# A schedule that counts buffer reuse and holds its DMA queue short, early buffers for the decay inputs, and a first batch mixed in single fp32 products

## The chip, the cores and the metric

The kernel runs on one core of a Trainium2 chip. The metric is device time in microseconds (us) for one execution. The engines are TensorE (PE, with its weight loads PEld), VectorE (DVE), ScalarE (ACT), GpSimd (POOL) and SyncE (SP), which here issues every DMA.

## The reference

Three blocks follow one another, for 4 batches, 768 time steps and 384 channels (8 heads of 48).

```python
# 1. attention with a decayed state, for each batch and head
f = 1.0 / (1.0 + np.exp(-f_logit))
for t in range(S):
    state = f[:, :, t, :, None] * state + np.einsum('bhd,bhe->bhde', k[:, :, t], v[:, :, t])
    y[:, :, t] = np.einsum('bhd,bhde->bhe', q[:, :, t], state)
# 2. token mix with phases
theta = x @ w_theta
zr, zi = x * np.cos(theta), x * np.sin(theta)
y = np.einsum('ts,bsd->btd', w_tok_r, zr) + np.einsum('ts,bsd->btd', w_tok_i, zi)
u = x + y
x = u + np.maximum(u @ w_ch, 0.0)
# 3. gated block with a spatial product
h = np.maximum(x @ w_in, 0.0); u, v = halves of h
v_n = (v - mean(v)) / sqrt(var(v) + 1e-6)
out = (u * (einsum('ts,bsd->btd', w_spatial, v_n) + b_spatial)) @ w_out
```

The token weights (w_tok_r, w_tok_i) arrive as 64-bit numbers and are turned into fp32 on the chip.

## The kernel before, in words

**Decays** (`dense`). The channels of one batch make three groups of 128 rows, so there are twelve groups, f0, k0, q0 to f11, k11, q11. For each group the kernel loads f, k and q (128x768), forms 1 + exp(-f) on ACT, takes a running product over chunks of 64 steps on DVE (the scan `icp<-f,one`), then multiplies k and q by what ACT makes of it by Ln and Exp. Before the scan a memset on GpSimd clears the first column of every chunk. The f tiles have one buffer (`BUFS`), the k and q tiles two each.

**Attention** (`att_load`, `att_k`, `att_w`, `att_s`, `att_x`). A unit is a pair of heads. Its rows are copied by DMA from the k and q tiles into `kp` and `qa`, and small products follow: scores `psc`, chunk states `pw`, outputs `px`. Two units have buffers at a time, and batch 0 has units 0 to 3.

**Phases** (`p1_theta`, `p1_z`). Per 128 time steps: theta (`pth`) on PE, its reduction on DVE, two sines on ACT, and z = x cos, x sin.

**Token mix** (`p1_acc`). `acc` sums z times token tiles over six blocks c of 128 steps, once for each half (th) of the output steps. With fp32r operands a product is made as three products over split operands (high x high, high x low, low x high); each operand's low part costs one ACT copy and one DVE subtraction (`split`). The token tiles of a batch are twelve, 128x768 each. In the first batch they are loaded raw (768 KB), decoded (one ACT and three DVE operations), and kept in DRAM for the later batches, either whole (`tkd`) or as two split parts (`tkp`). For b = 0 and c < MIX1 = 3 nothing is split: one fp32 product, which the profile counts as two records, stands for the three. Then z has one buffer in use and its second (`z10`, `z11`, `z12` of tags `z1c`) is idle until the second batch.

**Channel product** (`p1_u`, `p1_h`) follows each half, then block 3 for each batch (`pv`, `pu`, `pg`, `po`), all in triple products.

**What sets the order.** Up to the end of block 2 all instructions are recorded first. `Plan.schedule` then gives each engine a fixed order: a list schedule with a cost for each instruction, in which a unit takes a free buffer and waits for the earliest one. `late` computes from the end backwards by when each instruction must start, and these due times are the priorities of the next of four rounds; the best round's order is imposed. On the chip each engine runs its list strictly in order, SP its DMA issues too.

Names in rows and orders: `f1_221` is the f tile of group 1, `kp0`, `qa00` and `qa01` belong to even units and `kp1`, `qa10`, `qa11` to odd ones, `ws` is a raw load, `wb` a decoded tile that is split afterwards, `tk0` and `tk1` are token tiles (high or whole, and low).

Of the kernel before, what the change touches and what calls it, by code (L numbers as in the profile page):

```python
# [10 lines left out]
F32 = mybir.dt.float32  # L11
# [10 lines left out]
P = 128  # L22
B, H, S, D = 4, 8, 768, 48
# [3 lines left out]
NC = S // C  # L27
# [5 lines left out]
LIMIT = float(2.0**40)  # L33
TWO_PI = 2.0 * math.pi

THETA1, MIX1 = 2, 3

PARTS = 4
BUFS = {"f": 1, "k": 2, "q": 2}

FILL = 30

# [13 lines left out]


MODE, HOP, ISSUE, RATE, NARROW, LAND, SLACK = 0.1, 0.11, 0.6, 310e3, 160e3, 1.2, 0.05
ROUNDS = 4


# [27 lines left out]
class Plan:  # L89
# [111 lines left out]
            u[0].touch = {x for o in u for x in {b.t for b in o.out + o.src} if x in self.use}  # L201

    def schedule(self):
        free = {k: [0.0] * n for k, n in self.size.items()}
        turn = {k: 0 for k in self.order}
        left = {t: len(s) for t, s in self.use.items()}
        last = {t: 0.0 for t in self.use}
        queue = {e: [] for e in "TVAGQ"}
        for u in self.units:
            queue[u[0].e].append(u)  # L210
        for q in queue.values():
            q.sort(key=lambda u: (u[0].pri, u[0].i))
        now = {e: 0.0 for e in "TVAGQ"}
        end, seq, picks = {}, {e: [] for e in "TVAGQ"}, {}
        dma, mode, func, cols = 0.0, None, None, {}

        def ready(u):
            t, o = 0.0, u[0]
            for d, same in o.deps:
                x = end.get(d)  # L220
                if x is None:
                    return None
                t = max(t, x - HOP if same else x)
            for k, xs in o.need:
                f = free[k]
                if len(f) < len(xs):
                    return None
                i = turn[k]
                if self.order[k][i : i + len(xs)] != xs:
                    return None  # L230
                t = max(t, sorted(f)[len(xs) - 1])
            return t

        for _ in self.units:
            best = None
            for e in "TVAGQ":
                c = None
                for u in queue[e]:
                    r = ready(u)
                    if r is None:  # L240
                        continue
                    s = max(r, now[e])
                    if c is None or s < c[0] - 1e-9:
                        c = (s, u)
                    if s <= now[e] + SLACK:
                        break
                if c is not None and (best is None or c[0] < best[0]):
                    best = (c[0], e, c[1])
            s, e, u = best
            queue[e].remove(u)  # L250
            for k, xs in u[0].need:
                for _ in xs:
                    free[k].remove(min(free[k]))
                turn[k] += len(xs)
            t = s
            for o in u:
                o.start = t
                if e == "T":
                    if o.mode != mode and mode is not None:
                        t += MODE  # L260
                    mode = o.mode
                    if o.mode[1] < P and o.name != "transpose":
                        c = o.out[0].p[0]
                        x = max(t, cols.get(c, 0.0))
                        cols[c] = x + 2 * o.cost
                        t = x + 0.006
                        end[o] = cols[c] + HOP + 0.07
                    else:
                        t = max([t] + list(cols.values())) + o.cost
                        cols = {}  # L270
                        end[o] = t + HOP + 0.07
                elif e == "Q":
                    t += o.cost
                    dma = max(dma, t + 0.5) + o.bytes / o.rate
                    end[o] = dma + LAND
                else:
                    if o.func == "sin":
                        t += 0.1 + (1.28 if func != "sin" else 0)
                    func = o.func or func
                    t += o.cost  # L280
                    end[o] = t + HOP
                seq[e].append(o)
                for x in {b.t for b in o.out + o.src}:
                    if x in left:
                        left[x] -= 1
                        last[x] = max(last[x], end[o])
                        if not left[x]:
                            free[self.tag[x]].append(last[x])
            now[e] = max([t] + list(cols.values())) if e == "T" else t
        return max(now["T"], now["V"]), seq, end  # L290

    def late(self, seq, end):
        late = {}
        after = {}
        for e in "T":
            for x, y in zip(seq[e], seq[e][1:]):
                after[x] = y
        succ = {}
        for u in self.units:
            for d, same in u[0].deps:  # L300
                succ.setdefault(d, []).append((u[0], same))
        fin = max(end.values())
        for o in sorted(self.ops, key=lambda o: -o.start):
            t = fin
            for s, same in succ.get(o, ()):
                if s in late:
                    t = min(t, late[s] - (0 if same else HOP))
            if o in after and after[o] in late:
                t = min(t, late[after[o]])
            late[o] = t - (end[o] - o.start if o.e == "Q" else o.cost)  # L310
        return late

    def run(self):
        self.prepare()
        best = None
        for _ in range(ROUNDS):
            t, seq, end = self.schedule()
# [42 lines left out]
class Kernel:  # L360
# [105 lines left out]
    def dense(self, b, g):  # L466
        V, A, G = self.V, self.A, self.G
        self.ln_exp()
        n, t = 3 * b + g, {}
        self.dn[n] = t  # L470
        for x in ("f", "k", "q"):
            t[x] = self.a2.tile([P, S + NC], F32, name=f"{x}{n}", tag=x, bufs=BUFS[x])
            self.Q.dma_start(out=t[x][:, 0:S], in_=self.a[x].rearrange("u r t -> (u r) t")[P * n : P * n + P])
        f, k, q, cx = t["f"][:, 0:S], t["k"][:, 0:S], t["q"][:, 0:S], t["k"][:, S:]
        icp, cw = self.icp, self.cw
        fc = f.rearrange("p (c t) -> p c t", t=C)
        fs = self.a2.tile([P, NC], F32, name=f"fs{n}", tag="fs")
        self.act(f, f, AF.Exp, scale=-1.0)
        A.activation(f, f, AF.Copy, bias=1.0)
        V.reciprocal(fs, fc[:, :, 0])  # L480
        G.memset(fc[:, :, 0:1], 0.0)
        V.tensor_tensor_scan(icp, f, self.one.rearrange("p c t -> p (c t)"), 0.0, op0=ALU.mult, op1=ALU.add)
        G.tensor_copy(self.ge[:, n, :], icp[:, C - 1 : S : C])
        self.act(cw, icp, AF.Ln)
        self.act(cw, cw, AF.Exp, scale=-1.0)
        yield
        V.tensor_tensor(k, k, icp, op=ALU.mult)
        V.tensor_tensor(icp, cw, icp, op=ALU.mult)
        V.scalar_tensor_tensor(cw, icp, 2.0, cw, op0=ALU.subtract, op1=ALU.mult, reverse0=True)
        yield  # L490
        V.tensor_tensor(q, q, cw, op=ALU.mult)
        ce = cw.rearrange("p (c t) -> p c t", t=C)[:, :, C - 1]
        G.tensor_tensor(cx[:, 0 : NC - 1], ce[:, 0 : NC - 1], fs[:, 1:NC], op=ALU.mult)
        G.memset(cx[:, NC - 1 : NC], 0.0)
        yield
# [539 lines left out]
    def run(self):  # L1035
# [21 lines left out]
        dense = lambda b, g: self.ahead(self.dense(b, g), 1000 if g or b else 0)  # L1057
        w = self.p1_weights()
        run(dense(0, 0))
        run(take(w, NJ))  # L1060
        p = self.bank("pt")
        for _ in range(FILL):
            self.T.matmul(p[:, 0:P], lhsT=self.ident, rhs=self.ident, start=True, stop=True)
        self.att_k(0, 0)
        run(merge((dense(0, 1), 9), (self.att_pe(0, X[0]), 6)))
        self.att_k(0, 1)
        run(merge((dense(0, 2), 9), (self.att_pe(1, X[0]), 6)))
        self.att_k(0, 2)
        run(pe(2))
# [95 lines left out]
```

## Time and profile before

| | us |
|---|---|
| median of 3 runs | 646.95 |
| lowest and highest run | 645.7, 651.62 |
| profiled execution, first to last instruction (its span) | 642.1 |
| PE busy in it | 605.7 (94%) |
| DVE busy in it | 427.4 (67%) |
| ACT busy in it | 346.0 (54%) |

The profiled execution has no time of its own beside its span; the fastest run is 3.6 us over that span, the median 4.9 us. Shares of busy time are averages over stages with different limits: the profile is to be read by stretches of 20 us, and in each by which engine the others wait for.

### The profile page before, as it was taken

To read this page: it belongs to the slowest core of one execution; us is meant where nothing else is said; L and a number is where in the kernel's file an instruction comes from. 1 tells how busy PE (TensorE), PEld (TensorE's weight loads), DVE (VectorE), ACT (ScalarE), POOL (GpSimd) and SP (SyncE) were. 2 spreads that over 40 slices of the span, in tenths; PEclk is the share of its full clock that TensorE was granted. 3 is DMA by queue.
4 is the path that set the end of the run, shared out by engine and by line. 5 is a ranking of instruction groups with operands and counts; after the bars stand their busy time and mean duration, and the time that the engine had idled before them with its cause. 6 is when DMAs were issued, how large, how long until landed. Compare 5 with 4: busy or idle time off the path is not lost.

```text
span 642.1 us, 12784 instructions
## 1 busy us (share of the span) xinstructions
PE 605.7 (94%) x5140; PEld 558.4 (87%) x5140; DVE 427.4 (67%) x757; ACT 346.0 (54%) x637; POOL 28.7 (4%) x76
## 2 busy tenths in 40 slices
PE   9577988899999999999799999999999999999996
PEld 8466657678899998999799998999899989999996
DVE  3898799995979977776697525775745174518250
ACT  3666886646887678865675204633541263126211
POOL 5110001000002000010000000000000000000000
PEclk9668996999999999999999999999999999999999
DMA  8787667996968999365665634341010100020002
GB/s 264 233 245 232 230 198 222 318 319 195 330 213 255 313 310 243 120 215 177 203 223 191 215 102 160 90 134 55 19 53 22 66 10 24 1 75 1 1 1 79
DMA packets 40963, 102.05 MB, mean 159 GB/s; under 512 B 5696, under 2 KB 11840, under 8 KB 40896
## 3 DMA queue, kind: packets, MB, share of 16 engines
q1 hardware_dynamic: 40896, 101.15, 50.0%
q8 instruction: 42, 0.69, 0.4%
q14 instruction: 25, 0.20, 0.1%
HBM read 71.17 MB, written 20.45 MB: 143 GB/s over the span
## 4 chain that ended last, share of the span: by engine, by line
PE 79%; DVE 8%; DMA 5%; ACT 4%; issue 1%; POOL 1%; SPq 0%; DVEq 0%; ACTq 0%; POOLq 0%
PE acc L339 19%; PE pg L339 16%; PE pu L339 8%; PE po L339 8%; PE pv L339 8%; PE pth L339 5%; PE hh L339 5%; PE px L339 4%; PE psc L339 3%; PE pt L339 2%; DVE icp L339 2%; PE pw L339 1%; DMA f<-f_dram 1%; DMA xs<-x2d 1%; DMA tkd<-wb 1%
## 5 line engine op out<-in xcount | busy, mean ns | idle before, releaser
L339 PE MATMUL acc<-tk,z 128*128 128x384 f32 x828 | 169.8, 357 | 0.8 <-DVE xt L339 0.8
L339 PEld LDWEIGHTS acc<-tk,z 128*128 128x128 f32 x828 | 144.1, 189 | 10.9 <-DVE xt L339 1.3
L339 PE MATMUL pg<-wp,vn 128*128 128x384 f32 x576 | 100.5, 334 | 0.0
L339 PEld LDWEIGHTS pg<-wp,vn 128*128 128x128 f32 x576 | 99.9, 188 | 0.0
L339 ACT ACTIVATE gt<-g 128x384 fp32r<-128x384 f32 x32 | 16.8, 527 | 63.4 <-DVE g L339 63.4
L339 PE MATMUL pu<-x,wi 128*128 128x384 f32 x288 | 50.7, 334 | 0.0
L339 PE MATMUL po<-wo,gt 128*128 128x384 f32 x288 | 50.6, 336 | 0.0
L339 PEld LDWEIGHTS pu<-x,wi 128*128 128x128 f32 x288 | 50.1, 188 | 0.3
L339 PEld LDWEIGHTS po<-wo,gt 128*128 128x128 f32 x288 | 50.0, 188 | 0.0
L339 PE MATMUL pv<-wi,x 128*128 128x512 f32 x216 | 49.8, 390 | 0.0
L339 PEld LDWEIGHTS pv<-wi,x 128*128 128x128 f32 x216 | 40.5, 188 | 8.3
L339 PE MATMUL hh<-uT,wc 128*128 128x384 f32 x216 | 42.0, 342 | 3.3 <-DVE sn L339 3.1
L339 DVE BATCH_NORM_STATS2 st<-vv 128x6 f32<-128x512 f32 x24 | 16.5, 692 | 42.5 <-ACT vv L339 42.5
L339 PEld LDWEIGHTS psc<-qa,kp 64*64 64x64 f32 x768 | 28.7, 150 | 16.1 <-issue 12.0
L339 PE MATMUL psc<-qa,kp 64*64 64x64 f32 x768 | 32.2, 238 | 11.0 <-DVE qa L339 5.3
L339 DVE TENSOR_TENSOR qa<-psc,mask 64x384 f32<-64x384 f32 x64 | 35.5, 555 | 10.0 <-PE psc L339 8.5
L339 PEld LDWEIGHTS hh<-uT,wc 128*128 128x128 f32 x216 | 37.5, 188 | 5.1 <-DVE sn L339 3.4
L339 PE MATMUL px<-vs,qa 128*64 128x48 f32 x768 | 35.5, 253 | 5.6 <-ACT vs L339 3.9
L339 PEld LDWEIGHTS px<-vs,qa 128*64 128x64 f32 x768 | 31.8, 159 | 10.2 <-ACT vs L339 4.8
L339 DVE TENSOR_TENSOR g<-pg,bs 128x384 f32<-128x384 f32 x32 | 17.7, 557 | 27.1 <-PE pg L339 27.0
L339 ACT ACTIVATE vs<-cb 64x528 f32<-64x528 f32 x24 | 23.8, 990 | 14.1 <-DVE cb L339 13.9
L339 ACT ACTIVATE sn<-sn 128x384 f32<-128x384 f32 x48 | 24.5, 516 | 7.8 <-DVE sn L339 7.5
(111 smaller groups left out, 914.6 us busy)
## 6 DMA issues: line engine op xcount, KB each, us to landing
tk<-tkp SPq DMA_DIRECT2D x48, 384.0 KB, 4.4
ws<-tok_dram SPq DMA_DIRECT2D x12, 768.0 KB, 5.7
tkp<-tk SPq DMA_DIRECT2D x20, 384.0 KB, 5.2
f<-f_dram SPq DMA_DIRECT2D x12, 384.0 KB, 4.7
k<-k_dram SPq DMA_DIRECT2D x12, 384.0 KB, 6.6
q<-q_dram SPq DMA_DIRECT2D x12, 384.0 KB, 7.1
vn<-vu_dram SPq DMA_DIRECT2D x16, 288.0 KB, 5.8
vs<-va_dram SPq DMA_DIRECT2D x32, 144.0 KB, 5.1
```

The lines of the kernel that those rows point to most:

```text
L339: r = f(*a, **k)
```

## The change

1. `MIX1` goes from 3 to 6: in the first batch all six blocks of both halves use single fp32 products. No z and no token tile is split in that batch, all twelve decoded token tiles go whole to DRAM, and all twelve are split, and their parts stored, in the second batch.
2. `EARLY`: f1, f2, k2 and q2 get their tiles in the second z buffers, which are idle now through the first batch. They no longer wait for f0's buffer, or for k0's and q0's.
3. The memset before the scan moves from GpSimd to DVE.
4. `schedule` remembers which tile a buffer was taken from, and `late` counts the user of a buffer as a successor of the instructions of its previous tile.
5. `LEAD`: the schedule does not place a DMA before its modelled queue is within 1.5 us of empty. This is a rule of the planner alone; nothing on the chip enforces it.

```diff
-THETA1, MIX1 = 2, 3
+THETA1, MIX1 = 2, 6
+EARLY = {("f", 1): "z10", ("f", 2): "z11", ("k", 2): "z12", ("q", 2): "z13"}
+LEAD = 1.5
...
-                c = None
+                c, at = None, max(now[e], dma - LEAD) if e == "Q" else now[e]
...
-                    free[k].remove(min(free[k]))
+                    f = min(free[k])
+                    free[k].remove(f)
+                    self.took.append((f[1], u[0]))
...
+        for t, o in self.took:
+            for d in self.use.get(t, ()):
+                succ.setdefault(d, []).append((o, False))
...
-            t[x] = self.a2.tile([P, S + NC], F32, name=f"{x}{n}", tag=x, bufs=BUFS[x])
+            w = S + NC if x == "k" else S
+            if (x, n) in EARLY:
+                t[x] = self.c1.tile([P, w], F32, name=f"{x}{n}", tag=EARLY[x, n])
+            else:
+                t[x] = self.a2.tile([P, w], F32, name=f"{x}{n}", tag=x, bufs=BUFS[x])
...
-        G.memset(fc[:, :, 0:1], 0.0)
+        V.memset(fc[:, :, 0:1], 0.0)
```

The plan changes the order on every engine. On SP, at the start of the program, the loads before, from the second on:

```order
L339 DMA k0_140<-k_dram 128x768
L339 DMA q0_142<-q_dram 128x768
L339 DMA k1_223<-k_dram 128x768
L339 DMA vn0_102<-vu_dram 128x576
L339 DMA q1_225<-q_dram 128x768
L339 DMA vs0_100<-va_dram 64x576 x2
L339 DMA vn1_103<-vu_dram 128x576
L339 DMA vs1_101<-va_dram 64x576 x2
L339 DMA ws_160<-wt_dram 128x768
L339 DMA ws_167<-wt_dram 128x768
L339 DMA f1_221<-f_dram 128x768
```

and now:

```order
L348 DMA k0_140<-k_dram 128x768
L348 DMA f1_221<-f_dram 128x768
L348 DMA q0_142<-q_dram 128x768
L348 DMA k1_223<-k_dram 128x768
L348 DMA vn0_102<-vu_dram 128x576
L348 DMA q1_225<-q_dram 128x768
L348 DMA f2_370<-f_dram 128x768
L348 DMA vs0_100<-va_dram 64x576 x2
L348 DMA k2_372<-k_dram 128x768
L348 DMA kp0_104<-k0_140 48x780 x2
```

f1 moves from the fourteenth issue to the third, f2 and k2 come before the first unit's copies, and the theta weights (`wt`) go behind them.

On DVE, at the start, from the end of group 0's decays on, before:

```order
L339 TENSOR_TENSOR q0_142<-q0_142,cw_99 128x768
L339 TENSOR_SCALAR ft0_159<-ws_160 128x384
L339 SCALAR_TENSOR_TENSOR ft0_159<-ws_160,ft0_159 128x384 x2
L339 TENSOR_SCALAR ft1_166<-ws_167 128x384
L339 SCALAR_TENSOR_TENSOR ft1_166<-ws_167,ft1_166 128x384 x2
L339 RECIPROCAL fs1_227<-f1_221 128x12
L339 SCALAR_TENSOR_TENSOR icp_98<-f1_221,one_95 128x768
L339 TENSOR_TENSOR k1_223<-k1_223,icp_98 128x768
L339 TENSOR_TENSOR qa00_106<-psc_249,mask_91 64x384
L339 TENSOR_TENSOR qa01_107<-psc_249,mask_91 64x384
```

and now:

```order
L348 SCALAR_TENSOR_TENSOR cw_99<-icp_98,cw_99 128x768
L348 RECIPROCAL fs1_227<-f1_221 128x12
L348 MEMSET f1_221 128x12
L348 SCALAR_TENSOR_TENSOR icp_98<-f1_221,one_95 128x768
L348 TENSOR_TENSOR q0_142<-q0_142,cw_99 128x768
L348 TENSOR_TENSOR k1_223<-k1_223,icp_98 128x768
L348 TENSOR_TENSOR icp_98<-cw_99,icp_98 128x768
L348 SCALAR_TENSOR_TENSOR cw_99<-icp_98,cw_99 128x768
L348 TENSOR_TENSOR q1_225<-q1_225,cw_99 128x768
L348 RECIPROCAL fs2_376<-f2_370 128x12
L348 MEMSET f2_370 128x12
L348 SCALAR_TENSOR_TENSOR icp_98<-f2_370,one_95 128x768
```

The decays of groups 0, 1 and 2 stand directly behind one another, and the decoding of the theta weights (`ft`) comes after them.

On DVE, late in the first half of the first batch's mix (`tk0_978` is now the token tile of block 3, `tk0_987` was it), before:

```order
L339 TENSOR_SCALAR wb_989<-ws_990 128x768
L339 SCALAR_TENSOR_TENSOR wb_989<-ws_990,wb_989 128x768 x2
L339 TENSOR_TENSOR z13_798<-sn_790,z03_797 128x768
L339 TENSOR_TENSOR sn_811<-sn_811,X0_135 128x768
L339 TENSOR_TENSOR tk1_988<-wb_989,tk0_987 128x768
```

and now:

```order
L348 TENSOR_TENSOR z04_815<-sn_808,X0_135 128x768
L348 TENSOR_TENSOR z05_828<-sn_821,X0_135 128x768
L348 TENSOR_TENSOR wc1_81<-wb_848,wc0_80 128x384
L348 RECIPROCAL fs4_910<-f4_904 128x12
L348 MEMSET f4_904 128x12
L348 SCALAR_TENSOR_TENSOR icp_98<-f4_904,one_95 128x768
L348 TENSOR_TENSOR k4_906<-k4_906,icp_98 128x768
L348 TENSOR_SCALAR tk0_978<-ws_979 128x768
L348 SCALAR_TENSOR_TENSOR tk0_978<-ws_979,tk0_978 128x768 x2
```

The two subtractions of each block (for z and for the token tile) are gone, and the decode writes the token tile itself, of which there are three buffers, where it wrote `wb`, of which there is one.

## Rows read from the trace of the kernel before

**Rows 1.** The page's busy times: us, share of the span, instructions.

```profile
span 642.1 us, 12784 instructions
PE 605.7 (94%) x5140; PEld 558.4 (87%) x5140; DVE 427.4 (67%) x757; ACT 346.0 (54%) x637; POOL 28.7 (4%) x76
```

**Rows 2.** Stretches: length, PE, PEld, DVE, ACT, POOL busy (count), clock, DMA, GB/s.

```profile
0.00:20.00 20.00, 15.34 (x108) 14.99 (x108) 8.68 (x12) 8.10 (x11) 9.31 (x27) 1.00 0.85 249
38.77:65.07 26.30, 21.12 (x407) 18.58 (x410) 23.05 (x34) 17.02 (x36) 1.46 (x6) 0.81 0.78 244
65.07:118.72 53.65, 46.82 (x425) 34.98 (x417) 48.30 (x65) 40.69 (x68) 3.78 (x8) 0.90 0.73 233
118.72:167.41 48.69, 48.06 (x564) 37.92 (x564) 40.19 (x58) 28.79 (x52) 1.49 (x6) 1.00 0.88 276
...
200.00:220.00 20.00, 19.81 (x264) 17.92 (x264) 18.87 (x25) 15.77 (x24) 2.47 (x7) 1.00 0.94 280
220.00:240.00 20.00, 19.86 (x329) 18.23 (x325) 14.98 (x22) 13.04 (x26) 1.72 (x6) 1.00 1.04 314
```

**Rows 3.** Timeline of DVE: start, us, operation, out<-in, count [idle before <-releaser].

```profile
5.64 0.23 DVE L339 RECIPROCAL fs<-f 128x12 f32<-128x12 f32 x1 [5.64 <-ACT f L339]
8.60 1.76 DVE L339 TENSOR_TENSOR_SCAN icp<-f,one 128x768 f32<-128x768 f32 x1 [2.74 <-POOL f L339]
...
20.14 0.23 DVE L339 RECIPROCAL fs<-f 128x12 f32<-128x12 f32 x1 [0.94 <-ACT f L339]
...
37.81 0.96 DVE L339 TENSOR_TENSOR q<-q,cw 128x768 f32<-128x768 f32 x1
...
65.07 0.55 DVE L339 SCALAR_TENSOR_TENSOR sn<-sn,pth 128x384 f32<-128x384 int32 x1 [0.24 <-ACT sn L339]
...
69.01 0.96 DVE L339 TENSOR_TENSOR z<-sn,X 128x768 f32<-128x768 f32 x1 [2.99 <-ACT sn L339]
...
118.72 1.48 DVE L339 TENSOR_TENSOR xt<-acc,xt 128x384 f32<-128x384 f32 x3
```

**Rows 4.** Timeline of ACT, the first group's two passes over f.

```profile
3.89 1.72 ACT L339 ACTIVATE f<-f 128x768 f32<-128x768 f32 x2 [1.79 <-DMA f<-f_dram]
```

**Rows 5.** The chain that ended last, pieces in order: start us, us, what.

```profile
11.17 7.13 DMA f<-f_dram
...
22.44 0.85 ACT cw L339
...
102.91 2.22 PE acc L339 x6
...
145.42 1.29 PE acc L339 x4
...
182.91 3.13 PE acc L339 x18
```

**Rows 6.** Groups by form on DVE: out<-in xcount | busy us, mean ns | idle before.

```profile
L339 DVE TENSOR_TENSOR z<-sn,z 128x768 fp32r<-128x768 f32 x21 | 19.9, 949 | 2.2 <-ACT z L339 2.1
...
L339 DVE TENSOR_TENSOR tk<-wb,tk 128x768 fp32r<-128x768 f32 x6 | 5.7, 953 | 0.0
```

**Rows 7.** Timeline of PE, three of its waits.

```profile
98.63 1.54 PE L339 MATMUL pt<-ident,k 128*128 128x128 f32 x6 [4.77 <-DVE k L339]
...
119.32 1.56 PE L339 MATMUL acc<-tk,z 128*128 128x384 f32 x4 [0.59 <-DVE xt L339]
...
313.07 3.40 PE L339 MATMUL hh<-uT,wc 128*128 128x384 f32 x18 [3.08 <-DVE sn L339]
```

**Rows 8.** DMA issues of the whole program: out<-in, count, KB each, median us to landing.

```profile
tk<-tkp SPq DMA_DIRECT2D x48, 384.0 KB, 4.4
tkp<-tk SPq DMA_DIRECT2D x20, 384.0 KB, 5.2
...
ws<-tkd SPq DMA_DIRECT2D x12, 384.0 KB, 4.3
...
tkd<-tk SPq DMA_DIRECT2D x6, 384.0 KB, 7.2
```

More of the change, by code (lines that the diff above doesn't have):

```diff
@@ L203, in schedule @@
     def schedule(self):
-        free = {k: [0.0] * n for k, n in self.size.items()}
+        free = {k: [(0.0, "")] * n for k, n in self.size.items()}
+        self.took = []
         turn = {k: 0 for k in self.order}
@@ L230, in ready @@
                     return None
-                t = max(t, sorted(f)[len(xs) - 1])
+                t = max(t, sorted(f)[len(xs) - 1][0])
             return t
@@ L241, in schedule @@
                         continue
-                    s = max(r, now[e])
+                    s = max(r, at)
                     if c is None or s < c[0] - 1e-9:
                         c = (s, u)
-                    if s <= now[e] + SLACK:
+                    if s <= at + SLACK:
                         break
@@ L287, in schedule @@
                         if not left[x]:
-                            free[self.tag[x]].append(last[x])
+                            free[self.tag[x]].append((last[x], x))
             now[e] = max([t] + list(cols.values())) if e == "T" else t
```

## The prediction

> **What bounds the kernel now.** I read the busy times first: PE is busy in 605.7 of 642.1 us [rows 1], which says that PE sets most of the time but not where it does not. The stretches tell that [rows 2]. From 118.72 to 167.41 us PE is busy in 48.06 of 48.69 us, and in 200 to 240 us in 39.67 of 40: there PE is the limit and nothing but less work on PE helps. Before 118.72 us it is otherwise. In 65.07 to 118.72 us DVE is busy in 48.30 of 53.65 us, in 38.77 to 65.07 us in 23.05 of 26.30, at a granted clock of 0.81 to 0.90 since PE has pauses; in the first 20 us DVE is busy in 8.68 only. So the program has a front that DVE sets, with an idle start, and a long rest that PE sets. The border is where DVE first adds the mix result to x, at 118.72 us [rows 3]: PE takes up the second half 0.6 us later, having waited for just that [rows 7]. What the front saves before this point is saved at the end; what PE gains in work behind it is paid in full.
>
> The timeline of DVE shows why its start is idle [rows 3]: the first scan waits 2.74 us for the memset on GpSimd, and the second group's reciprocal starts at 20.14 us, since f1 is issued only at 11.17 us, when f0's buffer is free, and lands 7.13 us later [rows 5].
>
> **The front, part by part.** I follow the new DVE order with durations of rows.
>
> Group 0: its reciprocal still starts at 5.64 us. The memset then stands on DVE. No row has it there; the reciprocal of the same 128x12 elements takes 0.23 us [rows 3], nothing is the other end, and I take 0.1 (0.6 for the six groups of the front, within the sums below). The scan starts at 6.0 instead of 8.60 us. With 1.76 us for it, 0.96 for each multiplication [rows 3] and 0.85 each for Ln and Exp on ACT [rows 5], the last thing group 1 needs DVE to finish is done at 11.5 us.
>
> Group 1: f1 is now the third load. The first lands at 3.89 us [rows 4]; at the 249 GB/s of the first 20 us [rows 2] a 0.393 MB tile takes 1.6 us, so f1 lands at about 7.1. ACT is free for it at 9.5 and needs 1.72 us [rows 4]. Its reciprocal starts at 11.5 us, 8.6 earlier than now. Scan to 13.6, Ln and Exp to 15.3 beside two multiplications, q1 done at 18.4.
>
> Group 2: f2 is the eighth load (about 3.1 MB, landed near 14 us). Scan from 18.7 to 20.5, then some six operations of unit 0 and group 2's k (4.6 us), then its last three (2.9 us): q2 is done at 28 us. Now it is done at 37.81 + 0.96 = 38.8 [rows 3]. That is 10.8 us earlier.
>
> From q2 to the first reduction of theta (`sn`, 65.07 us): the stretch before holds 34 DVE operations, 23.05 us in 26.30 [rows 2]. The new order has 38 in the same place, by the same durations 0.3 us more. With the same idle time `sn` would start at 54.6 us. But less other work now lies between the waits for PE: unit 1's outputs come after unit 0's, unit 2's copies after those, and PE's order of units has not changed. I add 2.4 us of waiting and take 57, so 8 us of the 10.8 stay.
>
> From `sn` to the border: 65 operations, 48.30 us in 53.65 [rows 2]. Six subtractions of 0.95 us (three z, three token tiles) [rows 6] go, 5.7 us; one more token decode and part of the channel weights' decoding move in, so the net is 0.5 us less. The one long wait, 2.99 us for the first sines [rows 3], stays. The border moves from 118.7 to about 110.2 us: **8.5 us saved**. PE's pause of 4.77 us for k of a later group [rows 7] lies in this stretch; DVE sets it, and it is not counted again.
>
> **Single products.** A record of an fp32 product takes 1.29/4 = 0.322 us, two make 0.645; a triple takes 3 x 3.13/18 = 0.522 [rows 5]. So each of 36 products, 18 in each half, costs 0.123 us more. The first 18 lie in the front that DVE sets, where even the slow form there (2.22/6 = 0.37 us per record at the lower clock [rows 5]) leaves PE idle; they cost nothing unless DVE no longer covers them (up to 3.9 us). The other 18 lie behind the border: **2.2 us lost**. The Trainium skill, page "FP8 and Floating Point Precision", section "Matmul Precision", speaks against this edit: true fp32 makes four passes through the array; by four times 0.174 a product would cost 0.70 us, the second half 3.1 us more instead of 2.2, and the sum below would come out 0.9 us higher. The rows at 0.645 decide.
>
> **Fewer splits, more bytes.** Nine z and token subtractions on DVE and as many copies on ACT leave the first batch: behind the border this is worth nothing, PE covers it (DVE 40.19, ACT 28.79 of 48.69 us [rows 2]). `tkd` writes go from 8 to 12 (six are in [rows 8]) and `tkp` writes from 20 to 24, while reads stay at 12 and 48 [rows 8]. That is 8 x 0.393 = 3.1 MB more, and the second batch gets as much: 24 `tkp` writes instead of 12, 4 `tkd` reads more, 8 `tk` reads fewer. Between nothing (PE waits 0.33 us in 200 to 240 us while DMA's share is 0.94 and 1.04 [rows 2]) and 3.1 MB at the 297 GB/s of that stretch (10.6 us) I take nothing, as nearest to what that stretch shows.
>
> **The wait near 313 us**, 3.08 us of PE for DVE [rows 7], where ACT in its order waits for a late load of block 3: the new SP order has one pair of token loads fewer in front of that load. Between 0 and 3.1 us I take **0.5 saved**.
>
> **Due times and the short queue** have no instructions of their own. Their effect is the order, and that is what I followed.
>
> Sum: -8.5 + 2.2 - 0.5 = -6.8 us, a span of 635.3 instead of 642.1 us. The median of the runs lies 4.9 us over the span, so 640.2 us, 1.05% less. About 1% is what a measurement of this kernel can tell from no change, and the forecast lies right on that line.
>
> **The rivals.**
>
> *The front does not follow.* The copies of unit 0 now queue behind f2 and k2 (0.8 MB, 3.2 us at 249 GB/s), q0 comes one tile later, and the queue is short in the plan only: on the chip SP issues as fast as its order lets it. For this speaks a DMA share of 0.85 in the first 20 us [rows 2]; against it, that fewer bytes than now lie ahead of these copies, since the theta weights moved back. If the chain of units keeps half of the gain, the border moves by 4: -4 + 2.2 = -1.8, 645.2 us. Chance 0.20.
>
> *More is saved.* DVE waits no more in 38.77 to 65.07 us than now (`sn` at 54.6, 10.5 + 0.5 saved) and the wait of 3.1 us goes: -14.1 + 2.2 = -11.9, 635.0 us. For it, that DVE was busy in 88% of that stretch; against it, PE's unchanged order of units. Chance 0.18.
>
> *Slower: the second batch's token tiles wait for DMA.* Each of its twelve tiles is now read, split and written out in two parts before its buffer (one of three) is free. Six were so far. A block of the mix has 18 triples, 3.1 us of PE, and with the other work on PE about 7 us; a write lands after 5.2 us in the median [rows 8]. While a landing stays below what two more buffers cover, nothing happens; where the queue is full (1.04 in 220 to 240 us) the landings lengthen and PE starts to wait. The whole 3.1 MB at 297 GB/s is 10.6 us: 650.8 us, 0.6% slower, and beyond 1% if the front keeps half as well (655.8). Against it, that PE waits 0.33 us in the two stretches that hold such writes now, and that the first batch's load falls by 1.6 MB (four `tkd` writes more, eight `tkp` writes fewer). Chance 0.10.
>
> **How the numbers follow.** The forecast has 0.52, with its own range of 637 to 643.5; six tenths of it lie under 640.5, the line of 1%. Faster by over 1%: 0.31 + 0.18 = 0.49. Slower by over 1%: two thirds of the last rival, 0.07. Within 1%: the rest, 0.44. The range that should hold 8 in 10 goes from 633 (the second rival with a little less waiting) to 648 (the first rival with the first 18 products uncovered) and leaves out the last rival and the far side of the second.
>
> **What would show it.** The second reciprocal of DVE near 11.5 us, the first `sn` near 57, the first addition of `acc` near 110, and PE without pauses from there. Records of the mix at 0.322 us through the whole first batch. DMA at about 1.0 in the second batch without PE waiting for a token tile. I am wrong if `sn` comes after 61 us, if PE waits for DVE behind the border, or if token tiles hold PE in the second batch.

## The result and the profile after

The changed kernel took 642.25 us in the median of 4 runs, the kernel before 646.64 on the same chip: a ratio of 0.9897, with a 95% interval of 0.9852 to 0.9943. A second series gave 640.45 against 647.17 us, 0.9871 (0.9827 to 0.9915). The forecast was 640.2 us. Medians here are of all runs of a kernel, but the ratios leave out executions in a slower state (in the first series of the change the profiled one), so the rows below are those of the second series' profile unless the text says otherwise.

Busy times of the change, as in [rows 1]:

```profile
span 638.2 us, 12673 instructions
PE 606.0 (95%) x5104; PEld 551.7 (86%) x5104; DVE 417.8 (65%) x760; ACT 338.2 (53%) x628; POOL 23.1 (4%) x64
```

PE is as busy as before. DVE loses 9.6 us: three z and six token subtractions are gone, as the first of these two groups by form shows (18 instead of 21; `tk<-wb,tk` has left the view [rows 6]), and the second is the memset's new place:

```profile
L348 DVE TENSOR_TENSOR z<-sn,z 128x768 fp32r<-128x768 f32 x18 | 17.0, 949 | 4.3 <-ACT z L348 4.3
...
L348 DVE MEMSET f<- 128x12 f32 x12 | 0.8, 68 | 0.9
```

The timeline of DVE answers to [rows 3]:

```profile
5.81 0.23 DVE L348 RECIPROCAL fs<-f 128x12 f32<-128x12 f32 x1 [5.81 <-ACT f L348]
6.12 0.07 DVE L348 MEMSET f<- 128x12 f32 x1
6.29 1.76 DVE L348 TENSOR_TENSOR_SCAN icp<-f,one 128x768 f32<-128x768 f32 x1
...
11.76 0.22 DVE L348 RECIPROCAL fs<-f 128x12 f32<-128x12 f32 x1
...
28.05 0.96 DVE L348 TENSOR_TENSOR q<-q,cw 128x768 f32<-128x768 f32 x1
...
57.91 0.55 DVE L348 SCALAR_TENSOR_TENSOR sn<-sn,pth 128x384 f32<-128x384 int32 x1
...
110.76 1.48 DVE L348 TENSOR_TENSOR xt<-acc,xt 128x384 f32<-128x384 f32 x3
```

The second reciprocal comes 8.4 us earlier, q2 is done at 29.0 instead of 38.8, the first `sn` comes at 57.9 instead of 65.1 and the border at 110.76 instead of 118.72 us. So 8.0 us are gained in front of the border, and 6.7 us (series medians) or 3.9 (spans of the two profiles, 642.1 to 638.2) at the end. The two figures differ because the profile of the kernel before is of an execution shorter than most: the spans of its runs in the second series have a median of 645.1 us, those of the change 638.7. The stretches of the change, cut at its own first `sn` and border, for [rows 2], and PE's waits behind the border, for [rows 7]:

```profile
0.00:20.00 20.00, 15.63 (x161) 15.36 (x165) 11.76 (x17) 10.83 (x14) 9.94 (x29) 0.95 0.84 261
...
57.91:110.76 52.85, 46.82 (x433) 30.23 (x425) 47.61 (x69) 37.19 (x67) 2.57 (x6) 1.00 0.83 239
110.76:160.00 49.24, 46.91 (x468) 33.24 (x469) 40.02 (x60) 31.73 (x55) 1.54 (x5) 1.00 0.84 269
200.00:220.00 20.00, 18.32 (x311) 16.52 (x308) 15.45 (x24) 15.08 (x25) 0.20 (x1) 0.91 0.79 260
220.00:240.00 20.00, 20.00 (x202) 19.03 (x202) 15.19 (x24) 17.86 (x35) 1.04 (x3) 1.00 0.88 283
```

```profile
111.47 0.88 PE L348 MATMUL psc<-qa,kp 64*64 64x64 f32 x22 [0.82 <-DMA qa<-q]
121.99 0.93 PE L348 MATMUL psc<-qa,kp 64*64 64x64 f32 x23 [1.46 <-ACT X L348]
...
208.14 0.91 PE L348 MATMUL psc<-qa,kp 64*64 64x64 f32 x22 [1.40 <-DMA qa<-q]
...
304.31 4.97 PE L348 MATMUL hh<-uT,wc 128*128 128x384 f32 x18 [2.62 <-DVE sn L348]
```

Behind the border PE waits for scores (`psc`), and what releases two of these waits is a copy into `qa`. In all it waits 7.2 us between the border and the first product of block 3 (`pv`), where it waited 6.9 before. How PE's time up to `pv` divides shows what the 8.0 us are worth (the first row is of before, the second of the change):

```profile
0.00:387.44 387.44, 356.59 (x3772) 318.20 (x3773) 298.73 (x433) 250.08 (x430) 28.75 (x76) 0.96 0.74 231
```

```profile
0.00:382.63 382.63, 356.56 (x3737) 311.53 (x3738) 289.20 (x436) 242.42 (x421) 23.11 (x64) 0.96 0.78 242
```

PE is as long busy as before and idle for 26.1 us instead of 30.9, so the 4.8 us by which `pv` comes earlier are all idle time. Of the 8.0 us at the border 5.1 are idle time of PE (23.9 to 18.8 us); the other 2.9 are busy time, and behind the border PE is busy for 2.85 us more. The DMA issues, for [rows 8], have the 24 `tkp` and 12 `tkd` writes that were counted:

```profile
tk<-tkp SPq DMA_DIRECT2D x48, 384.0 KB, 3.9
...
tkp<-tk SPq DMA_DIRECT2D x24, 384.0 KB, 5.1
...
tkd<-tk SPq DMA_DIRECT2D x12, 384.0 KB, 5.5
...
ws<-tkd SPq DMA_DIRECT2D x12, 384.0 KB, 4.3
```

### The profile page after: what moved, and what is told of

It is laid out like the page before. It is cut to its first block, busy times and chain, and to the rows that moved or that the text cites. A ratio compares the mean times of both kernels' runs of the same rounds, so it can differ in the third digit from the quotient of the medians.

```text
span 645.9 us, 12673 instructions
## 1 busy us (share of the span) xinstructions
PE 610.2 (94%) x5104; PEld 554.7 (86%) x5104; DVE 417.8 (65%) x760; ACT 338.4 (52%) x628; POOL 23.1 (4%) x64
## 2 busy tenths in 40 slices
DMA packets 42114, 105.18 MB, mean 163 GB/s; under 512 B 5824, under 2 KB 11968, under 8 KB 42048
## 3 DMA queue, kind: packets, MB, share of 16 engines
HBM read 71.17 MB, written 23.59 MB: 147 GB/s over the span
## 4 chain that ended last, share of the span: by engine, by line
PE 76%; DVE 9%; DMA 8%; ACT 3%; issue 2%; SPq 1%; POOL 0%; DVEq 0%; ACTq 0%
PE acc L348 22%; PE pg L348 15%; PE po L348 8%; PE hh L348 6%; PE pu L348 6%; PE pv L348 6%; PE pth L348 5%; PE px L348 4%; PE psc L348 3%; DMA wb<-wp_dram 3%; DMA ws<-tok_dram 3%; PE pt L348 2%; DVE icp L348 2%; DVE qa L348 1%; DMA qa<-q 1%
## 5 line engine op out<-in xcount | busy, mean ns | idle before, releaser
L348 PE MATMUL acc<-tk,z 128*128 128x384 f32 x792 | 175.5, 372 | 0.4 <-DVE tk L348 0.4
L348 PEld LDWEIGHTS acc<-tk,z 128*128 128x128 f32 x792 | 139.7, 190 | 17.8 <-DVE tk L348 1.0
L348 PE MATMUL hh<-uT,wc 128*128 128x384 f32 x216 | 44.6, 359 | 3.3 <-DVE sn L348 3.0
L348 PEld LDWEIGHTS hh<-uT,wc 128*128 128x128 f32 x216 | 40.7, 201 | 4.7 <-DVE sn L348 3.3
L348 PE MATMUL px<-vs,qa 128*64 128x48 f32 x768 | 33.7, 249 | 4.9 <-ACT vs L348 3.2
L348 ACT ACTIVATE ws<-ws 128x768 f32<-128x768 f32 (+2 forms) x28 | 20.5, 739 | 18.6 <-DMA ws<-tok_dram 11.3
L348 PE MATMUL pth<-ft,xt 128*128 128x384 f32 x72 | 25.5, 493 | 3.7 <-ACT xt L348 3.7
```

What stands on the lines that cost most here:

```text
L348: r = f(*a, **k)
```

## The experiments

The theory after the result was the prediction's own: the front is earlier because f1 and f2 load early. Its rivals were that the gain is the missing splits, or that it is the two rules of the planner (called here the queue rule, `LEAD`, and the reuse rule, the due times through `took`). The change has three parts that can be made apart: the single products, the early buffers (the memset on DVE goes with them, but for mix_plan_v) and the rules. Each run is planned anew, so it differs from the others in its whole order and not only in the part that its edit names. All numbers stand in one table; "border" is the first `xt<-acc`, with two times where the three operations of the group fall apart; marks are from the profiled execution of each.

| run | single products | early buffers | rules | us, median (n) | ratio, 95% interval | first `sn` | border | first `pv` |
|---|---|---|---|---|---|---|---|---|
| before | | | | 646.6 to 647.2 | 1 | 65.07 | 118.72 | 387.44 |
| again | yes | yes | both | 640.45 (6) | 0.9871 (0.9827 to 0.9915) | 57.91 | 110.76 | 382.63 |
| mix_only | yes | | | 648.9 (12) | 1.0024 (0.9992 to 1.0055) | 66.61 | 107.68, 118.46 | 394.05 |
| early_only | | yes | | 655.14 (7) | 1.0108 (1.0070 to 1.0146) | | | |
| early_look | | yes | | 654.87 (1) | | 66.50 | 126.11, 127.32 | 397.74 |
| plan_only | | | both | 646.95 (12) | 0.9964 (0.9930 to 0.9999) | 61.95 | 120.29 | 388.48 |
| early_plan | | yes | both | 641.12 (8) | 0.9914 (0.9882 to 0.9946) | 58.47 | 119.20 | 383.26 |
| mix_plan | yes | | both | 635.42 (6) | 0.9814 (0.9781 to 0.9848) | 59.95 | 108.92, 110.25 | 375.07 |
| mix_plan_v | yes | | both | 639.48 (6) | 0.9897 (0.9856 to 0.9938) | 59.63 | 115.52 | 382.60 |
| mix_early | yes | yes | none | 649.6 (10) | 1.0044 (1.0020 to 1.0068) | 72.99 | 121.14 | 393.11 |
| no_lead | yes | yes | reuse | 646.47 (10) | 0.9997 (0.9969 to 1.0024) | 66.78 | 112.70, 115.09 | 389.22 |
| no_took | yes | yes | queue | 650.03 (10) | 1.0050 (1.0022 to 1.0079) | 60.46 | 113.99, 124.51 | 392.42 |
| land25 | yes | yes | both | 635.99 (7) | 0.9834 (0.9801 to 0.9867) | 60.51 | 110.07 | 376.39 |

### The change again, and each part alone

**again** is the change as it is.

> The change as it is, timed again. Theory A (the front set by DVE gets 8 us shorter; about half of that is lost behind it, where PE waits for DMA of attention copies and then runs at the lower clock): 0.5 to 1.5% faster, single runs as far apart as 635 to 648 us, and a profile in which the first reductions and the border stay near 57.9 and 110.7 us while the waits of PE behind 110 us (3.1 us near 111, 2.9 us near 209, 3.0 us near 308 in the first profile) differ in size. Rival B (the loss behind the border is fixed by the new order of PE and DVE): the same waits at the same places with the same sizes, runs within 0.5% of one another.

Its front is that of the first profile to 0.1 us (`sn` 57.91 and 57.89, border 110.76 and 110.73), so the front's marks repeat, while the waits behind the border differ (0.82 us for 3.14 near 111 us): theory A.

**mix_only** is the kernel before with one number changed.

```diff
-THETA1, MIX1 = 2, 3
+THETA1, MIX1 = 2, 6
```

> Only MIX1 = 6 in the kernel before, with the old plan, old buffers and the GpSimd memset. Theory A: the front loses six subtractions of DVE (5.7 us) but keeps its idle start of 14 us, the second half costs 2.2 us more: 643 to 647 us, 0 to 0.6% faster, second reciprocal of DVE still at 20 us. Rival C (the single products carry the change): 641 us or less, over 0.8% faster.

Nothing is gained: the same subtractions are gone, but the last part of the border stays at 118.46 us and the ratio is 1.0024. The median lies 1.9 us above what theory A allowed.

**early_only** is the kernel before with the early tiles and the memset on DVE; q2 stays where it was, since z13 is in use while `MIX1` is 3.

```diff
+EARLY = {("f", 1): "z10", ("f", 2): "z11", ("k", 2): "z12"}
...
-        G.memset(fc[:, :, 0:1], 0.0)
+        V.memset(fc[:, :, 0:1], 0.0)
```

> Only the early buffers (f1, f2 and k2 in the second z buffers of blocks 0 to 2; q2 stays in its pool, since block 3 needs its z buffer with MIX1 = 3) and the memset on DVE, with the old plan. Theory A: second reciprocal near 12 us, border 5 to 8 us earlier than 118.7, nothing paid for single products: 639 to 642 us, 0.8 to 1.2% faster. Rival B (the new plan carries it, the buffers do little without it): 644 to 648 us.

It is 1.1% slower, against the theory and beyond its rival too.

**plan_only** is the change with only its rules left.

```diff
-THETA1, MIX1 = 2, 6
+THETA1, MIX1 = 2, 3
...
-EARLY = {("f", 1): "z10", ("f", 2): "z11", ("k", 2): "z12", ("q", 2): "z13"}
+EARLY = {}
...
-        V.memset(fc[:, :, 0:1], 0.0)
+        G.memset(fc[:, :, 0:1], 0.0)
```

> Only the two planner rules (due times through buffer reuse, DMA placed within 1.5 us of an empty modelled queue), with MIX1 = 3, old buffers and the GpSimd memset. Theory A: the idle start stays, so 644 to 648 us, within 0.5% of before. Rival B: 642 us or less.

A ratio of 0.9964, hardly distinct from 1. No part carries the gain by itself, so it lies in their combination, and pairs had to be made.

### The parts in pairs

**early_look** is early_only once more, for a profile.

> The same kernel as early_only, for a profile that is not disturbed. Theory D (without the rule on the queue the old plan fills the early buffers at the cost of the first unit's copies, which stand behind 17 loads where the change has them behind 12): second reciprocal of DVE near 12 to 14 us, but scores of unit 0 on PE not before 22 us (19.9 in the kernel before) and the first sn at 65 us or later. Rival E (the front is shorter as in the change and the loss lies behind the border): first sn near 58 us.

PE's timeline shows a loss at the start. The first line is this kernel's, the second that of the change at the same place (the first scores of unit 0):

```profile
24.98 0.44 PE L341 MATMUL psc<-qa,kp 64*64 64x64 f32 x2 [9.84 <-POOL ge L341]
```

```profile
17.82 1.50 PE L348 MATMUL psc<-qa,kp 64*64 64x64 f32 x19 [2.84 <-DMA qa<-q]
```

The releaser that is named is a copy on POOL that ended at 24.85 us. Unit 0's large copies into `kp`, issued from 15.14 us on, took 9.1 us to land in the median and so ended at about the same time; this row alone doesn't decide between the two (under no_lead, below, it is the copies). The early tiles bring the second reciprocal to 14.72 us, and the first scores come 7.2 us later than in the change, and 7.0 later than in early_plan, below (17.97 us), which differs from this kernel by the rules alone.

**early_plan** is the change without its single products: early tiles and both rules.

```diff
-THETA1, MIX1 = 2, 6
+THETA1, MIX1 = 2, 3
-EARLY = {("f", 1): "z10", ("f", 2): "z11", ("k", 2): "z12", ("q", 2): "z13"}
+EARLY = {("f", 1): "z10", ("f", 2): "z11", ("k", 2): "z12"}
```

> Early buffers, memset on DVE and both planner rules, but MIX1 = 3 (so q2 without an early buffer): the change without its single products. Theory D (buffers and queue rule gain only together, and the single products cost): 634 to 641 us, 1 to 2% faster, border near 112 us. Rival C (the single products are needed, since they take six subtractions out of the front): 643 to 647 us.

Its first `sn` is nearly as early as in the change, 58.47 us, but its border is at 119.20, not near the 112 that theory D expected:

```profile
58.47:119.20 60.73, 50.27 (x523) 37.41 (x525) 56.02 (x80) 45.76 (x78) 3.58 (x6) 0.97 0.77 236
```

Between the two marks DVE is busy for 56.02 us, against 47.61 in the change: 5.8 of the 8.4 us more are the six subtractions, most of the rest is work on later units. More of PE's work on later units lies ahead of that border too, so it can't be laid beside the change's; from border to `pv` it takes 264.1 us, where before took 268.7, and the ratio is 0.9914. A border is a mark of order, not a fixed amount of work, and is compared only between kernels that have the same work ahead of it. On DVE the change, mix_plan, mix_plan_v and land25 have that, to within 0.5 us.

**mix_plan** is the change without the early buffers, and with the memset on GpSimd again.

```diff
-EARLY = {("f", 1): "z10", ("f", 2): "z11", ("k", 2): "z12", ("q", 2): "z13"}
+EARLY = {}
...
-        V.memset(fc[:, :, 0:1], 0.0)
+        G.memset(fc[:, :, 0:1], 0.0)
```

> Single products in the whole first batch and both planner rules, but the old buffers and the GpSimd memset. Theory D: the idle start is back (second reciprocal near 18 us), so 643 to 648 us. Rival F (the plan and the single products make the gain, the buffers are a trifle): 641 us or less.

It is the fastest of all, 635.42 us, so theory D fell and F held. Against plan_only, from which it differs by the single products alone, the ratio falls from 0.9964 to 0.9814 and the border from 120.29 to 110.25: under the rules the single products are worth a good deal, under the old plan (mix_only) nothing. Its second reciprocal is at 17.16 us and its first `sn` at 59.95, 2.0 us later than in the change, and yet the border comes at 110.25:

```profile
59.95 0.55 DVE L348 SCALAR_TENSOR_TENSOR sn<-sn,pth 128x384 f32<-128x384 int32 x1
...
108.92 0.54 DVE L348 TENSOR_TENSOR xt<-acc,xt 128x384 f32<-128x384 f32 x1
...
110.25 1.00 DVE L348 TENSOR_TENSOR xt<-acc,xt 128x384 f32<-128x384 f32 x2
```

```profile
110.25:160.00 49.75, 49.75 (x543) 35.25 (x539) 41.48 (x60) 32.76 (x58) 2.27 (x6) 1.00 0.85 280
200.00:220.00 20.00, 20.00 (x306) 18.50 (x302) 18.37 (x26) 18.08 (x29) 1.29 (x5) 1.00 0.87 283
```

Behind the border PE is busy without a pause in both stretches, 49.75 of 49.75 and 20.00 of 20.00 us; the change has 46.91 of 49.24 and 18.32 of 20.00, at a DMA share that is no higher (0.84 to mix_plan's 0.85, then 0.79 to 0.87) and with the same bytes in all (105.18 MB in both pages).

**mix_early** is the change without both rules.

```diff
-                c, at = None, max(now[e], dma - LEAD) if e == "Q" else now[e]
+                c, at = None, now[e]
...
-        for t, o in self.took:
-            for d in self.use.get(t, ()):
-                succ.setdefault(d, []).append((o, False))
```

> Single products, early buffers and the memset on DVE with the old plan: the change without its two planner rules. Theory D: the first unit's copies stand behind too many loads again, 648 to 656 us, as slow as early_only or a little slower than before. Rival G (the rules only polish): 639 to 643 us.

The gain is gone, 1.0044. The first scores start at 26.06 us after a wait of 9.76 us for `qa`, and the first `sn` comes at 72.99. Fewer splits and early tiles are worth nothing, or less, under the old plan.

### Each rule, the memset, and the waits behind the border

Two questions were left: whether the early buffers make the change slower than mix_plan (H in these texts; by its rival, I, the memset on DVE does), and which rule does what.

**mix_plan_v** leaves the memset on DVE and takes only the early buffers out.

```diff
-EARLY = {("f", 1): "z10", ("f", 2): "z11", ("k", 2): "z12", ("q", 2): "z13"}
+EARLY = {}
```

> The change without its early buffers, but with the memset on DVE (mix_plan had it on GpSimd). Theory H (the early buffers cost more than they bring, since the order that they lead to makes PE wait for attention copies behind the border): 633 to 637 us, PE without waits between 120 and 300 us. Rival I (the memset on DVE is what makes the change slower than mix_plan): 639 to 642 us.

0.9897, within the intervals of the change's two series. So at the end the early buffers neither cost nor bring anything that can be told here, though the border is 4.8 us later than in the change: `pv` comes at the same time, since PE is idle for 27.0 us up to it, where it was for 26.1 in the change.

```profile
0.00:382.60 382.60, 355.65 (x3736) 310.74 (x3737) 289.39 (x436) 243.32 (x421) 25.81 (x64) 0.96 0.78 242
```

Against mix_plan only the engine of the memset differs, the border moves from 110.25 to 115.52 us, and the ratio by 0.8%, as rival I expected. That can't be the memset's 0.07 us apiece: the plan came out in another order. Why so far was not found. It means that a difference of 0.8% between two of these runs can come from the new order alone, whatever the edit.

**land25** is the change with a plan that reckons with later landings: `LAND` is the time that the schedule adds between the modelled end of a transfer and its use.

```diff
-MODE, HOP, ISSUE, RATE, NARROW, LAND, SLACK = 0.1, 0.11, 0.6, 310e3, 160e3, 1.2, 0.05
+MODE, HOP, ISSUE, RATE, NARROW, LAND, SLACK = 0.1, 0.11, 0.6, 310e3, 160e3, 2.5, 0.05
```

> The change with the plan's landing time of a DMA raised from 1.2 to 2.5 us; nothing else. Attention copies landed 3.6 to 4.9 us after their issue in the second profile of the change (again). Theory J (PE waits behind the border because the plan takes copies for landed too early): the waits for qa and kp near 111, 121 and 207 us shrink to under 1 us in all, 634 to 638 us. Rival K (the waits are a matter of the queue's order and not of the time that the plan assumes): waits of the same size elsewhere, 638 to 643 us.

635.99 us, with the early buffers in and the border at 110.07. The stretches behind it and PE's one long wait there:

```profile
110.07:160.00 49.93, 49.69 (x506) 35.01 (x498) 42.12 (x63) 34.08 (x59) 1.38 (x5) 1.00 0.86 273
200.00:220.00 20.00, 20.00 (x295) 18.70 (x295) 17.01 (x24) 18.25 (x30) 1.36 (x3) 1.00 0.89 292
```

```profile
298.32 4.91 PE L348 MATMUL hh<-uT,wc 128*128 128x384 f32 x18 [2.93 <-DVE sn L348]
```

The waits for copies behind the border are gone, as theory J has it, and with them H. Its copies don't land sooner (the 24 large ones into `kp` in 4.2 us in the median, against 3.8 in the change), so the plan must have placed them or what uses them otherwise; which of the two was not isolated, and by what mix_plan_v showed the gain itself may be luck of the order.

**no_lead** takes the queue rule out alone.

```diff
-                c, at = None, max(now[e], dma - LEAD) if e == "Q" else now[e]
+                c, at = None, now[e]
```

> The change without the rule on the short queue; due times through buffer reuse stay. Theory L (the queue rule carries the plan's part): copies of unit 0 behind many loads again, first sn at 65 us or later, 646 to 654 us. Rival M (due times carry it): 638 to 643 us.

The whole gain goes, 0.9997. Its stretch from 8 to 26 us, the DMA issues of that stretch (the four columns are tiles, count, KB, us to landing) and PE's first scores:

```profile
8.00:26.00 18.00, 7.54 (x67) 7.22 (x67) 16.28 (x23) 11.92 (x17) 4.66 (x10) 0.78 0.97 275
```

```profile
kp<-k SPq DMA_DIRECT2D x3, 146.2 KB, 8.8
qa<-q SPq DMA_DIRECT2D x3, 144.0 KB, 6.2
```

```profile
25.27 0.44 PE L348 MATMUL psc<-qa,kp 64*64 64x64 f32 x2 [10.28 <-DMA kp<-k]
```

and the same stretch of the change:

```profile
8.00:26.00 18.00, 12.24 (x167) 11.56 (x167) 15.65 (x21) 11.57 (x18) 3.29 (x9) 0.78 0.78 222
```

```profile
kp<-k SPq DMA_DIRECT2D x4, 146.2 KB, 3.3
qa<-q SPq DMA_DIRECT2D x3, 144.0 KB, 2.9
```

SP issues unit 0's first copy at 15.07 us instead of 12.21, 2.9 us later, and a copy into `kp` then takes 8.8 us to land instead of 3.3. In the 7 us before the first copy SP issues seven loads here, 2.2 MB, by an estimate 7.9 us at the stretch's 275 GB/s, and 0.5 MB in the change. mix_early and early_look, which have early buffers and no queue rule either, have landings of 8.0 and 9.1 us; under land25, which has the rule, the share is as high (1.00) and the copies take 5.6. So a busy queue alone does not make 8.8 us; the loads issued ahead of the copies would account for it. The Trainium skill, page "DMA: Bandwidth & Descriptors", section "Queues, rings and completion order", says that a DMA engine takes the descriptors of one ring in their order; the two landing times (8.8 and 3.3 us) agree with that, a small copy paying for what stands ahead of it.

**no_took** takes the reuse rule out alone.

```diff
-        for t, o in self.took:
-            for d in self.use.get(t, ()):
-                succ.setdefault(d, []).append((o, False))
```

> The change without due times through buffer reuse; the queue rule stays. Theory L: 637 to 643 us. Rival M: 646 us or more.

1.0050. Here the front's start is good (`sn` at 60.46), but the border's last part is at 124.51, and in the second batch PE stands still:

```profile
213.84 1.54 PE L345 MATMUL psc<-qa,kp 64*64 64x64 f32 x24 [6.09 <-ACT X L345]
```

The queue rule alone thus mends the start (its first scores come at 18.37 us, copies into `kp` land in 2.7), and the gain is lost later. So L fell for this run as M did for no_lead: it takes both rules. How the reuse rule prevents such a wait was not isolated.

## Why the prediction was right, and where its account was not

**The sum held, in part by luck.** It was -6.8 us; the second series has -6.7, the first -4.4. The marks on the way held to about 1 us: 11.5, 28, 57 and 110.2 us were expected, 11.76, 29.0, 57.91 and 110.76 came. But between the two profiles the sum is -3.9 us: -8.0 at the border, 2.85 more of PE's busy time and 0.3 more of its waiting from there to `pv`, and 0.9 behind `pv`. The change's span is 638.2 us where 635.3 was forecast, and its median lies 2.25 us above the span where 4.9 was taken over from before; the two errors cancel.

**The step that failed is the front's attribution.** The prediction booked 8 us to f1 and f2 loaded early ("so 8 us of the 10.8 stay") and 0.5 to the missing splits. Stretches of the two kernels up to the first `sn` and the runs without each part say otherwise:

```profile
0.00:65.07 65.07, 47.98 (x735) 43.88 (x738) 48.91 (x68) 37.86 (x68) 14.86 (x39) 0.82 0.80 243
```

```profile
0.00:57.91 57.91, 45.10 (x759) 41.45 (x761) 44.08 (x64) 35.47 (x64) 11.60 (x35) 0.82 0.80 235
```

Before it, DVE was busy for 48.91 us and idle for 16.2; now it is busy for 44.08 and idle for 13.8. So of the 7.2 us, 4.8 are work that was put behind `sn` (the decoding of one token tile and part of that of the channel weights, about 2.5 us each), and only 2.3 are idle time saved. That work has to be done before the border all the same, and it fits there because the six subtractions (5.7 us) left it: 48.30 us of DVE between the marks before [rows 2], 47.61 now. Over the whole front DVE has 5.5 us less to do (91.7 instead of 97.2 us) and is idle 2.4 us less; that is the 8.0 us. The runs agree at `sn`: with the rules alone it comes at 61.95, with the single products too at 59.95, with the early buffers too at 57.91, where they were to bring 8 us and bring 2.0 (3.5 between plan_only and early_plan). At the border it is open what they bring: without them it comes at 110.25 (mix_plan) or at 115.52 (mix_plan_v), with them at 110.76. At the end the runs without them are no slower. My net of 0.5 was a difference of two terms, work in and work out, and I took the small net for a small cause.

**The border is not passed on.** The prediction says that "what the front saves before this point is saved at the end". mix_plan_v has the same DVE work ahead of a border 4.8 us later than the change's, and the same `pv` (382.60 and 382.63 us). What counted for the most part was the idle time of PE up to `pv`, wherever it lay: 30.9 us before, 26.1 and 27.0 in these two, 21.1 in mix_plan.

**The rules were priced too low.** I gave them no cost of their own, only the order that I followed. That order is theirs: without the queue rule, or the reuse rule, or both, the same three edits of the program give 0.9997, 1.0050 and 1.0044. The rival that the front does not follow, since "the queue is short in the plan only", fell for the change: the imposed order did keep the queue short on the chip (landings of 3.3 us). It is the true account of no_lead and mix_early.

**Single products** cost what the records said. The chain of the change shows them behind the border:

```profile
127.35 1.29 PE acc L348 x4
130.22 1.29 PE acc L348 x4
```

0.322 us per record, 0.645 per product, where the rule of four passes that the prediction weighed (the Trainium skill, page "FP8 and Floating Point Precision", section "Matmul Precision") would give 0.70 by an estimate, four times 0.174. PE is busy for 264.64 us from border to `pv`, 2.85 more than before (261.79), where 2.2 were expected for the products. The difference was not taken apart, and the two stretches don't hold quite the same small products; part of the stretch ran at a lower granted clock (0.91 in 200 to 220 us).

**More bytes** cost nothing that shows: 23.59 MB are written to HBM instead of 20.45, PE waits for no token tile in the second batch, and mix_plan writes the same bytes with PE idle for 1.8 us only from border to `pv`. The rival that was to end slower fell.

**The wait near 313 us** went from 3.08 to 2.62 us, 0.46 saved where 0.5 was taken; in the first profile of the change it is 3.02, so this small term is not shown.

**What I left out:** "PE without pauses from there" did not come true. PE waits 7.2 us from border to `pv`, as much as before, and 2.2 of them (0.82 and 1.40) for copies into `qa`. Waiting is the larger part of the 7.6 us between the first `pv` of the change and that of mix_plan: 0.5 at the border, 5.4 of waiting (7.2 against 1.8), and 1.7 of PE time (264.64 against 262.99). In the medians the two better plans, mix_plan and land25, stand 5.0 and 4.5 us below the change; the intervals of their ratios and the change's still touch. Both come to the 635 us of the rival "more is saved", but not on its way: their `sn` is later than the change's.

## What to carry to other kernels

Where two edits move one mark, count the busy and the idle time of the engine that sets it, up to that mark, in both kernels: an earlier mark may only mean that work was put behind it. Free buffers can do harm if the planner does not know that a load in the queue delays the small copies behind it; under the old plan the early buffers cost 1.1%, and under the rules no clear gain of theirs shows. And when a list schedule sets the order, every edit draws a new order: moving twelve memsets of 0.07 us to another engine shifted the ratio by 0.8%. So take one part out in more than one way before you price it, and try the model's own constants too (a longer landing time gave 0.9834 against 0.9871, with intervals that touch).

## What the runs showed of the hardware

Copies of 144 to 146 KB between tiles in SBUF landed in 2.7 to 9.1 us in the median of a stretch, the long times where many loads were issued ahead of them; the issue of those into `kp` took SP 0.53 to 0.57 us each in the median of the first 40 us, with single ones up to 1.06.

A short wait of PE can cost as much again. In the change PE waits 1.40 us ahead of 208.14 us, and then the granted clock is 0.64 for 3.86 us, by an estimate 1.4 us of PE's time; after a wait of 1.46 us ahead of 121.99 us it stays at 1.00 (last row):

```profile
206.44:208.14 1.70, 0.30 (x2) 0.16 (x2) 1.59 (x3) 1.65 (x4) 0.00 (x0) 1.00 0.97 257
208.14:212.00 3.86, 3.86 (x32) 3.79 (x33) 3.21 (x5) 2.41 (x4) 0.20 (x1) 0.64 1.04 412
...
121.99:128.00 6.01, 5.85 (x69) 5.43 (x70) 4.55 (x7) 2.80 (x5) 0.00 (x0) 1.00 0.99 335
```

In the first profile of the change PE waits 3.14 us for `kp`, and the 5 us that follow run at 0.50, which is the lower of the clock's two levels, 1.2 GHz:

```profile
110.00:115.00 5.00, 1.86 (x70) 1.63 (x66) 2.21 (x4) 2.43 (x6) 0.00 (x0) 0.86 0.99 233
115.00:120.00 5.00, 5.00 (x44) 3.20 (x40) 2.47 (x3) 3.24 (x7) 0.00 (x0) 0.50 0.96 321
```

The same order of instructions, with the same border to 0.03 us, reached `pv` at 389.74 us there and at 382.63 in the second profile. The 24 large copies into `kp` took 4.7 us to land in the median there and 3.8 in the second; whether that is the cause was not tested.
